# Attention and a two-layer feed-forward on one core: two score blocks side by side, one more PSUM bank for part of the first product, and loads of values begun elsewhere

## The chip, the cores and the metric

The kernel runs on one core of a Trainium2 chip. Its time is the device time of one execution in microseconds; the median of three runs is used. TensorE (PE in the profile) multiplies, VectorE (DVE) and ScalarE (ACT) work on its results, GpSimd (POOL) masks and starts loads, and SyncE (SP) starts transposing and storing transfers. All times here are microseconds unless another unit stands with them.

## The reference

Attention with 4 batches, 8 heads, 768 positions and 64 values a head. Each query sees its last 128 keys and the first 4 keys, the sinks. Its result, 3072 tokens of 512 numbers, goes through two products with a GELU of the sigmoid form between them:

```python
keep = is_sink | in_window
scores = np.where(keep, scale * np.matmul(q, k.transpose(0, 1, 3, 2)), -1e9)
a = np.exp(scores - np.max(scores, axis=-1, keepdims=True))
a = a / (np.sum(a, axis=-1, keepdims=True) + 1e-09)
x = np.matmul(a, v)          # heads are put side by side: (3072, 512)
h = x @ w_in                 # (3072, 2048)
out = (h * (1 / (1 + np.exp(-1.702 * h)))) @ w_out
```

## The kernel before

**Tiles.** A group is 256 tokens of one batch: three groups a batch, 12 in all, g = 0 to 11. Within a group, the heads go in four pairs (hp = 0 to 3) and the queries in two blocks of 128 (i). The position of the group within its batch is t = g mod 3; at t = 0 the first block has no block of keys ahead of it, so some work is smaller there.

**Steps of a group.** `load_qk` and `load_v` bring queries, keys and values as fp16 by transfers that POOL issues (L123). Queries and keys are transposed, from group 4 on by a transfer that SP issues (`transposed_qk`, L169). `sinks` computes the scores with the sink keys. `scores` computes one pair's scores into a PSUM tile `nat` of two banks: eight products that use 64 rows of the array each (L222, L224). `maxima` runs on DVE: it lays the previous block's allowed scores over the own block's (L236), takes maxima (L240) and makes the bias (L244). `weights` takes the exponentials on ACT (L255), `weights_transposed` transposes them by a transfer of SP (L275, tile `AT`), `lower` on DVE and `upper` on POOL mask them (L305, L318), `values` multiplies with the values (L332 to L344), and `normal` divides by the sums (L361, L362). `x_transposed` transposes the result by another transfer (L380). `hidden` computes one eighth of the first product (tile `hT`, eight products of 128x256) and its GELU (L397); `out_part` computes a quarter of the second product for one block of 128 tokens (four products of 128x512, L409), and `out_store` copies the result out of PSUM, on ACT for block 0 (L435) and on DVE for block 1 (L437).

**Stages.** The order is written out by hand. In stage n the attention of group n runs beside the first product of group n-1 and the second product of group n-2. `second` opens the stage: exponentials of pairs 0 and 1 on ACT, the second product of block 0, the scores of pair 2, a quarter of the second product of block 1, the scores of pair 3, and the other three quarters. Then come eight steps F2 = 0 to 7 of the first product, and between them the sinks' transpose and the scores of pairs 0 and 1 of group n+1 (F2 = 1), and the value products of the four pairs (F2 = 3, 4, 6, 7). Each engine works through its instructions in the order in which the code issues them.

**PSUM.** It has eight banks: `nat` has two buffers of two banks; the pool "mm" has two banks, for `hT` and the second product's `o`, which take turns; the pool "av" has two, for the sinks' transpose `tAs`, the sinks' scores `sk` and the value products. In stage 11, which has the first product of group 10 (NG - 2), `hidden` takes av banks for F2 = 2 and 3.

**Loads.** The queries and keys of group n+3 are issued in stage n, each load behind one of the masks of POOL. The two loads of values of group n+3 are issued in stage n too, each after a copy of one number on POOL (`paced_load`, L352) that waits for the reciprocals of pair 1 and of pair 2. The values of group 4 are loaded before stage 2.

Of the kernel before, what the change touches and what calls it, by code (L numbers as in the profile page):

```python
# [57 lines left out]
def kernel(  # L58
# [11 lines left out]
    nc = tc.nc  # L70
# [6 lines left out]
    NF = DF // P  # L77
    NT = S // TG
    NG = B * NT
# [15 lines left out]
    pace = big.tile([1, 1], FP32, name="pace")  # L95
# [13 lines left out]
    G = [dict() for _ in range(NG)]  # L109

    def load_part(g: int, part: int):


        b, t = divmod(g, NT)
        e, i = divmod(part, 2)
        rows = slice(t * TG + i * P, t * TG + (i + 1) * P)
        if part == 0:
            G[g]["qkn"] = work.tile([P, 4, DM], FP16, tag="qkn", bufs=3, name=f"qkn{g}")
        if part < 4:
            dst = G[g]["qkn"][:, part].rearrange("s (h d) -> s h d", h=H)  # L120
        else:
            dst = vn[b][t][:, i, :, 0:D]
        nc.gpsimd.dma_start(dst, (q, k, v)[e][b, :, rows].rearrange("h s d -> s h d"))  # L123
# [5 lines left out]
    def load_v(g: int):  # L129
        for part in (4, 5):  # L130
            load_part(g, part)
# [77 lines left out]
    def scores(g: int, hp: int):  # L209

        b, t = divmod(g, NT)
        qkT = G[g]["qkT"]
        nat = psp.tile([P, 2, 2, 2 * P], FP32, tag="nat", bufs=2, name=f"nat{g}_{hp}")
        for i in range(2):
            I = 2 * t + i
            prev = None if I == 0 else qkT[:, 1, 0, hp] if i else G[g - 1]["qkT"][:, 1, 1, hp]
            for part, keys in ((0, prev), (1, qkT[:, 1, i, hp])):
                for h in range(2):
                    r = bass.ts(h, D)
                    o = nat[:, h, i, bass.ts(part, P)]  # L220
                    if keys is None:
                        nc.tensor.matmul(o, masked_l[r], masked_r[r], start=True, stop=True)  # L222
                    else:
                        nc.tensor.matmul(o, qkT[r, 0, i, hp], keys[r], start=True, stop=True)  # L224
        G[g]["nat", hp] = nat

    def kinds(mask, t: int):

        m = mask.rearrange("p (i c) -> p i c", i=2)
        if t == 0:  # L230
            return m.unsqueeze(1).broadcast_to((P, 2, 2, P))
        return m[:, 1:2].unsqueeze(1).broadcast_to((P, 2, 2, P))

    def maxima(g: int, hp: int):
        nat = G[g]["nat", hp]
        nc.vector.copy_predicated(  # L236
            out=nat[:, :, :, P:], mask=kinds(take_prev, g % NT), data=nat[:, :, :, 0:P]
        )
        m1 = work.tile([P, 2, 2], FP32, tag="m1", name=f"m1{g}_{hp}")
        nc.vector.tensor_reduce(  # L240
            out=m1.rearrange("p h i -> p (h i)"), in_=nat.rearrange("p h i c -> p (h i) c")[:, :, P:],
            axis=AX.X, op=ALU.max,
        )
        nc.vector.scalar_tensor_tensor(  # L244
            out=G[g]["bias"][:, :, hp], in0=m1.rearrange("p h i -> p i h"), scalar=-scale,
            in1=G[g]["m2"][:, :, hp], op0=ALU.mult, op1=ALU.min,
        )
# [13 lines left out]
    def weights_transposed(g: int, hp: int):  # L261
        A = G[g]["A", hp]
        AT = work.tile([P, 2, 2, P], FP16, tag="AT", bufs=6, name=f"AT{g}_{hp}")
        flat = AT.rearrange("p h i s -> p (h i) s")
        if g < 3:
            bank = av_bank if g == 2 or (g, hp) == (1, 3) else mm_bank
            tp = bank(f"tA{g}_{hp}", (P, 4, P), FP16)
            for a in range(4):
                nc.tensor.transpose(tp[:, a], A[:, a], ident)
            if g == 0 or hp < (2 if g == 2 else 3):  # L270
                nc.scalar.copy(flat, tp)
            else:
                nc.vector.tensor_copy(out=flat, in_=tp)
        else:
            nc.sync.dma_start_transpose(flat, A.rearrange("p a c -> p (a c)"))  # L275
        G[g]["AT", hp] = AT
# [69 lines left out]
                )  # L346
        G[g]["av", hp] = av

    def paced_load(g: int, part: int, n: int, hp: int):

        if g < NG:
            nc.gpsimd.tensor_copy(out=pace, in_=G[n]["rcp", hp][0:1, 0, 0:1])  # L352
            load_part(g, part)

    def normal(g: int, hp: int):
        av = G[g]["av", hp]
# [27 lines left out]
    def hidden(g: int, F2: int):  # L384
        xT = G[g]["xT"]
        if F2 == 0:
            G[g]["gT"] = work.tile([P, NF, TG], FP16, tag="gT", bufs=3, name=f"gT{g}")

        bank = av_bank if g == NG - 2 and F2 in (2, 3) else mm_bank
        hT = bank(f"hT{g}_{F2}", (P, 2, 2, P))  # L390
        for f in range(2):
            F = 2 * F2 + f
            for c in range(4):
                nc.tensor.matmul(  # L394
                    hT[:, f], w_in16[:, c, bass.ts(F, P)], xT[:, :, c], start=(c == 0), stop=(c == 3)
                )
        nc.scalar.activation(  # L397
            out=G[g]["gT"][:, 2 * F2 : 2 * F2 + 2].rearrange("p f s -> p (f s)"),
            in_=hT.rearrange("p f i s -> p (f i s)"),
            func=AF.Gelu_apprx_sigmoid,  # L400
        )

    def out_part(g: int, i: int, part: int):

        if part == 0:
            G[g]["o", i] = mm_bank(f"o{g}_{i}")
        o, gT = G[g]["o", i], G[g]["gT"]
        for F in range(4 * part, 4 * part + 4):
            nc.tensor.matmul(o, gT[:, F, bass.ts(i, P)], w_out16[:, F], start=(F == 0), stop=(F == NF - 1))  # L409

    def out_last(g: int, i: int):
# [82 lines left out]
    def o(g: int, i: int, *parts):  # L494
        if 0 <= g < NG:
            for p in parts:
                out_part(g, i, p)

    def valued(g: int, hp: int):
        values(g, hp)  # L500
# [65 lines left out]


    hidden(0, 0)
    weights_transposed(1, 3)
    lower(1, 3)  # L570
# [3 lines left out]
    load_v(2)  # L574
    load_v(3)
    load_qk(4)
    load_v(4)
    hidden(0, 1)
    sink_transposed(1)
    qk_block(2, 0, by_dve)  # L580
# [49 lines left out]
    def second(n: int, g2: int, att: bool):  # L630

        if att and n + 1 < NG and (n + 1) % NT == 0:
            sink_keys((n + 1) // NT, nc.gpsimd.tensor_copy)
        if att:
            for hp in (0, 1):
                weights(n, hp)
                weights_transposed(n, hp)
        o(g2, 0, 0, 1, 2, 3)
        if att:
            scores(n, 2)  # L640
            maxima(n, 2)
        if g2 == NG - 1:
            out_store(g2, 0)
            out_last(g2, 1)
            return
        o(g2, 1, 0)
        if att:
            scores(n, 3)
            maxima(n, 3)
            sink_terms(n)  # L650
        o(g2, 1, 1, 2, 3)
        out_store(g2, 0)
        if att:
            weights(n, 2)
            weights_transposed(n, 2)
        out_store(g2, 1)
        if att:
            weights(n, 3)
            weights_transposed(n, 3)
            sink_weights(n)  # L660
            lower(n, 0)
            if n + 2 < NG:
                transposed_qk(n + 2)

    for n in range(2, NG + LAG2):
        att = n < NG
        g1, g2 = n - LAG1, n - LAG2

        if n > 2:
            second(n, g2, att)  # L670
        else:
            transposed_qk(n + 2)
        if att:
            if n > 2:
                upper(n, 0)
                upper(n, 1)
            for part in range(4):
                if n + 3 < NG:
                    load_part(n + 3, part)
                if n > 2 and part < 2:  # L680
                    upper(n, 2 + part)
        if n in (2, 3, 4):
            sink_columns(n - 1)

        for F2 in range(NF // 2):
            if 0 <= g1 < NG:
                hidden(g1, F2)
            if not att:
                continue
            if n == 2 and F2 == 0:  # L690
                weights_transposed(n, 3)
                upper(n, 3)
            if F2 == 1:
                sink_transposed(n)
                ahead(n + 1, 0)
                lower(n, 1)
                ahead(n + 1, 1)
            if F2 == 2:
                lower(n, 2)
            for hp, at in enumerate((3, 4, 6, 7) if n + 1 < NG else (4, 5, 6, 7)):  # L700
                if F2 == at:
                    values(n, hp)
                    if hp == 0:
                        lower(n, 3)
                    normal(n, hp)
                    if hp in (1, 2):
                        paced_load(n + 3, 3 + hp, n, hp)
        if att:
            x_transposed(n)
            if n + 1 < NG and (n + 1) % NT == 0:  # L710
                sink_values((n + 1) // NT)
# [34 lines left out]
```

## Time and profile before

| | |
|---|---|
| median of 3 runs | 242.43 (241.89 to 242.43) |
| the profiled execution | 242.06, of which the span is 240.3 |
| PE busy | 222.3 (93% of the span), 2220 instructions |
| ACT, DVE, POOL busy | 156.7, 147.3, 103.5 |
| hT products, L394 | 768, 95.6 busy |
| o products, L409 | 368, 85.3 busy |
| GELU, L397 | 96 of 597 ns |
| exponentials, L255 | 192 of 375 ns |
| loads of q, k and v, L123 | 72 of some 0.9 us on POOL, 5.5 to 6.2 to landing |
| DMA | 32.07 MB, 133 GB/s on average |

The busy time of PE counts each product from its start to a modelled end, and ends overlap the next starts; a product of 128x256 is shown with 275 ns though eight of them start within 0.87 us. So a share of 93% does not say that PE is near its peak, and a wait of a tenth of a microsecond is seen only in the distance between two starts. A timeline row gives the start from the beginning of the span, the duration, the engine, the line of the kernel, the operation, what it writes and reads, the shape and the number of merged instructions; brackets tell how long the engine was idle before it and what ended that.

The stages start at their first o product: stage 3 at 61.45, then 78.22, 95.85, 113.14, 129.96, 147.24, 164.92, 181.74, and stage 11 at 199.39. Each is 16.3 to 17.7 long.

### The profile page before, as it was taken

What the parts mean: (1) busy time and instruction counts of PE and PEld (TensorE: products, weight loads), DVE (VectorE), ACT (ScalarE), POOL (GpSimd) and SP (SyncE); (2) the same over time, 40 slices, a digit from 0 to 9 for tenths busy, and PEclk for the clock granted to TensorE, in tenths of its full rate; (3) what the DMA queues carried; (4) which work ended last, traced back from release to release, by engine and by line L of the source; (5) the groups of instructions that cost most, each with busy time, mean ns of one, the idle gap of its engine ahead of it and who ended that gap; (6) DMA issues with size and microseconds to landing.
All of it is one profiled execution on the core that took longest, in us unless ns stands there. A gap on an engine that the chain in (4) does not pass through costs nothing.

```text
span 240.3 us, 5810 instructions
## 1 busy us (share of the span) xinstructions
PE 222.3 (93%) x2220; PEld 155.6 (65%) x2220; DVE 147.3 (61%) x388; ACT 156.7 (65%) x356; POOL 103.5 (43%) x158
## 2 busy tenths in 40 slices
PE   1677799999999999999999999999999999999994
PEld 0454578569569469478487486585585685684863
DVE  4787947579478377477675585776692883840100
ACT  2297774884875775785776777667668658760531
POOL 8988484857237357257046057148020310310000
PEclk9999989999999999999999999999999999999999
DMA  9999999999999969989989999999982513503102
GB/s 81 148 193 193 176 207 178 154 142 148 115 154 193 137 157 172 134 158 160 151 142 153 156 165 133 172 138 125 138 196 54 148 21 65 152 5 87 46 0 87
DMA packets 130699, 32.07 MB, mean 133 GB/s; under 512 B 123120, under 2 KB 127728, under 8 KB 130672
## 3 DMA queue, kind: packets, MB, share of 16 engines
q0 software_dynamic: 79104, 13.64, 79.2%
q1 hardware_dynamic: 50992, 17.88, 41.3%
q8 instruction: 17, 0.28, 0.5%
q10 hardware_dynamic: 576, 0.20, 0.3%
q14 instruction: 10, 0.08, 0.1%
HBM read 27.50 MB, written 6.29 MB: 141 GB/s over the span
## 4 chain that ended last, share of the span: by engine, by line
PE 64%; DMA 16%; DVE 7%; ACT 5%; POOL 4%; issue 2%; SPq 1%; ACTq 0%; DVEq 0%; POOLq 0%
PE hT L394 28%; PE o L409 25%; DMA qkn<-in_k_dram 5%; DMA AT<-A 4%; DMA qkT<-qkn 4%; DMA w_in<-in_moe_w_in_dram 3%; POOL qkn L123 3%; DVE m L240 3%; DVE nat L236 3%; PE nat L224 2%; PE av L344 2%; ACT L397 2%; PE av L332 2%; PE av L340 2%; PE o L420 1%
## 5 line engine op out<-in xcount | busy, mean ns | idle before, releaser
L394 PE MATMUL hT<-xT,w_in 128*128 128x256 f16 x768 | 95.6, 275 | 1.4 <-ACT gT L397 0.9
L409 PE MATMUL o<-w_out,gT 128*128 128x512 f16 x368 | 85.3, 380 | 0.0
L397 ACT ACTIVATE gT<-hT 128x512 f16<-128x512 f32 x96 | 56.2, 597 | 41.2 <-PE hT L394 40.9
L394 PEld LDWEIGHTS <-w_in 128*128 128x128 f16 x768 | 72.8, 98 | 13.7 <-issue 1.1
L318 POOL TENSOR_SCALAR_AFFINE_SELECT up<-AT 128x512 f16<-128x512 f16 (+1 forms) x48 | 27.2, 574 | 93.6 <-DMA AT<-A 86.0
L255 ACT ACTIVATE A<-nat,bias 128x128 f16<-128x128 f32 x192 | 53.7, 375 | 18.9 <-DVE bias L244 17.3
L409 PEld LDWEIGHTS <-gT 128*128 128x128 f16 x368 | 33.6, 98 | 37.2
L236 DVE COPY_PREDICATED nat<-prev,nat 128x512 f32<-128x512 uint16 x48 | 33.3, 693 | 28.0 <-PE nat L224 17.9
L240 DVE TENSOR_REDUCE m<-nat 128x4 f32<-128x512 f32 x48 | 33.2, 691 | 1.6
L123 POOL DMA_DIRECT2D vn<-in_v_dram x24 | 21.3, 895 | 5.3 <-DMA w_out<-in_moe_w_out_dram 4.0
L123 POOL DMA_DIRECT2D qkn<-in_q_dram x24 | 21.6, 908 | 1.4 <-POOLq L727 0.8
L123 POOL DMA_DIRECT2D qkn<-in_k_dram x24 | 21.3, 893 | 2.2 <-DMA w_in<-in_moe_w_in_dram 1.7
L362 DVE TENSOR_TENSOR xn<-av,rcp 128x256 f16<-128x256 f32 x48 | 20.4, 425 | 1.7
L305 DVE TENSOR_TENSOR lo<-AT,own 128x512 f16<-128x512 f16 (+1 forms) x48 | 18.7, 412 | 2.3 <-DMA AT<-A 2.3
L340 PE MATMUL av<-vn,up 128*128 128x65 f16 x160 | 18.3, 195 | 0.0
L344 PE MATMUL av<-vn,lo 128*128 128x65 f16 x160 | 18.3, 196 | 0.0
L361 DVE RECIPROCAL rcp<-av 128x4 f32<-128x4 f32 x48 | 8.6, 179 | 14.6 <-PE av L344 14.5
L332 PE MATMUL av<-vs,AsT 128*128 128x130 f16 x80 | 16.5, 224 | 0.5 <-DVE qkT L153 0.3
L224 PEld LDWEIGHTS <-qkT 64*128 64x128 f16 x352 | 11.7, 100 | 7.4 <-issue 6.6
L224 PE MATMUL nat<-qkT 64*128 64x128 f16 x288 | 16.5, 232 | 0.0
L340 PEld LDWEIGHTS <-up 128*128 128x128 f16 x160 | 14.8, 100 | 1.2 <-issue 0.4
L397 ACT ACT_TABLE_LOAD x11 | 14.1, 1283 | 0.2
(58 smaller groups left out, 179.3 us busy)
## 6 DMA issues: line engine op xcount, KB each, us to landing
out_dram<-osb SPq DMA_DIRECT2D x23, 256.0 KB
qkn<-in_q_dram POOLq DMA_DIRECT2D x24, 128.0 KB, 5.6
qkn<-in_k_dram POOLq DMA_DIRECT2D x24, 128.0 KB, 5.5
vn<-in_v_dram POOLq DMA_DIRECT2D x24, 128.0 KB, 6.2
w_in<-in_moe_w_in_dram POOLq DMA_DIRECT2D x4, 512.0 KB, 9.9
w_out<-in_moe_w_out_dram POOLq DMA_DIRECT2D x4, 512.0 KB, 12.4
AT<-A SPq DMA_TRANSPOSE x36
xT<-xn SPq DMA_TRANSPOSE x10
```

The costliest lines, as they stand in the source:

```text
L123: nc.gpsimd.dma_start(dst, (q, k, v)[e][b, :, rows].rearrange("h s d -> s h d"))
L224: nc.tensor.matmul(o, qkT[r, 0, i, hp], keys[r], start=True, stop=True)
L236: nc.vector.copy_predicated(out=nat[:, :, :, P:], mask=kinds(take_prev, g % NT), data=nat[:, :, :, 0:P])
L240: nc.vector.tensor_reduce(out=m1.rearrange("p h i -> p (h i)"), in_=nat.rearrange("p h i c -> p (h i) c")[:, :, P:], axis=AX.X, op=ALU.max,)
L255: nc.scalar.activation(out=A[:, 2 * h + i], in_=nat[:, h, i, P:], func=AF.Exp, bias=bias[:, i, hp, h : h + 1], scale=scale,)
L318: nc.gpsimd.affine_select(out=out, in_=in_, pattern=[[0, rows], [-1, P]], compare_op=ALU.is_gt, fill=zero_reg, base=0, channel_multiplier=1,)
L332: nc.tensor.matmul(av[:, i].rearrange("p h d -> p (h d)"), AsT, vs[b][:, c : c + 2].rearrange("p h d -> p (h d)"), start=True, stop=False,)
L340: nc.tensor.matmul(av[:, i, h], up[:, h, i], vn[b][J // 2][:, J % 2, head], start=False, stop=False)
L344: nc.tensor.matmul(av[:, i, h], own_w[:, h, i], vn[b][t][:, i, head], start=(I == 0), stop=(I == 0 or h == 1))
L394: nc.tensor.matmul(hT[:, f], w_in16[:, c, bass.ts(F, P)], xT[:, :, c], start=(c == 0), stop=(c == 3))
L397: nc.scalar.activation(out=G[g]["gT"][:, 2 * F2 : 2 * F2 + 2].rearrange("p f s -> p (f s)"), in_=hT.rearrange("p f i s -> p (f i s)"), fun ...
L409: nc.tensor.matmul(o, gT[:, F, bass.ts(i, P)], w_out16[:, F], start=(F == 0), stop=(F == NF - 1))
```

## The change

Three edits. In `second`, the scores of pair 2 and pair 3 are issued one right behind the other, after two products of block 1 instead of before its first quarter and after it; the maxima of both follow. In `hidden`, the step F2 = 2 takes its bank from "av" instead of "mm" for groups 2 to 9 (group 10 keeps F2 = 2 and 3). And the values of group n+2 (instead of n+3) are loaded in `second` of stage n, behind one copy on POOL that waits for the last exponential of pair 1; the values of group 4 are loaded in stage 2, behind its loads of queries and keys. `out_part` takes a range of products instead of the number of a quarter.

```diff
-    def paced_load(g: int, part: int, n: int, hp: int):
+    def paced_values(g: int, n: int):
         if g < NG:
-            nc.gpsimd.tensor_copy(out=pace, in_=G[n]["rcp", hp][0:1, 0, 0:1])
-            load_part(g, part)
+            nc.gpsimd.tensor_copy(out=pace, in_=G[n]["A", 1][0:1, 3, 0:1])
+            load_v(g)
...
-        bank = av_bank if g == NG - 2 and F2 in (2, 3) else mm_bank
+        more = (2,) if 2 <= g < NG - 2 else (2, 3) if g == NG - 2 else ()
+        bank = av_bank if F2 in more else mm_bank
...
     load_qk(4)
-    load_v(4)
     hidden(0, 1)
...
             for hp in (0, 1):
                 weights(n, hp)
                 weights_transposed(n, hp)
+            paced_values(n + 2, n)
         o(g2, 0, 0, 1, 2, 3)
-        if att:
-            scores(n, 2)
-            maxima(n, 2)
...
-        o(g2, 1, 0)
+        out_part(g2, 1, 0, 2)
         if att:
+            scores(n, 2)
             scores(n, 3)
+            maxima(n, 2)
             maxima(n, 3)
             sink_terms(n)
-        o(g2, 1, 1, 2, 3)
+        out_part(g2, 1, 2, NF)
...
+        if n == 2:
+            load_v(4)
...
-                    if hp in (1, 2):
-                        paced_load(n + 3, 3 + hp, n, hp)
```

More of the change, by code (lines that the diff above doesn't have):

```diff
@@ L401, in hidden, with out_part @@
         )
-    def out_part(g: int, i: int, part: int):
-        if part == 0:
+    def out_part(g: int, i: int, F0: int, F1: int):
+        if F0 == 0:
             G[g]["o", i] = mm_bank(f"o{g}_{i}")
         o, gT = G[g]["o", i], G[g]["gT"]
-        for F in range(4 * part, 4 * part + 4):
+        for F in range(F0, F1):
             nc.tensor.matmul(o, gT[:, F, bass.ts(i, P)], w_out16[:, F], start=(F == 0), stop=(F == NF - 1))
@@ L496, in o @@
             for p in parts:
-                out_part(g, i, p)
+                out_part(g, i, 4 * p, 4 * p + 4)
     def valued(g: int, hp: int):
```

## The prediction

> **What bounds the kernel now.** I read the page first, then the PE timeline of one stage, then DVE, ACT and POOL in the same stretch.
>
> ```profile
> PE 222.3 (93%) x2220; PEld 155.6 (65%) x2220; DVE 147.3 (61%) x388; ACT 156.7 (65%) x356; POOL 103.5 (43%) x158
> ...
> PE 64%; DMA 16%; DVE 7%; ACT 5%; POOL 4%; issue 2%; SPq 1%; ACTq 0%; DVEq 0%; POOLq 0%
> ```
>
> TensorE carries 64% of the chain that ended last, and no other engine comes near. Its ends are modelled, so a short stall does not show as idle; it shows between starts. Stage n=6 (113.14 to 129.96), PE alone:
>
> ```profile
> 113.14 3.62 PE L409 MATMUL o<-w_out,gT 128*128 128x512 f16 x16
> 116.69 0.23 PE L222 MATMUL nat<-maskedr,maskedl 64*128 64x128 f16 x2
> 116.76 0.33 PE L224 MATMUL nat<-qkT 64*128 64x128 f16 x6
> 117.02 1.04 PE L409 MATMUL o<-w_out,gT 128*128 128x512 f16 x4
> 117.99 0.23 PE L222 MATMUL nat<-maskedr,maskedl 64*128 64x128 f16 x2
> 118.06 0.33 PE L224 MATMUL nat<-qkT 64*128 64x128 f16 x6
> 118.32 2.76 PE L409 MATMUL o<-w_out,gT 128*128 128x512 f16 x12
> 120.92 1.98 PE L394 MATMUL hT<-xT,w_in 128*128 128x256 f16 x16
> ...
> 123.07 0.23 PE L224 MATMUL nat<-qkT,qkT 64*128 64x128 f16 x2
> ...
> 123.30 0.22 PE L224 MATMUL nat<-qkT,qkT 64*128 64x128 f16 x2
> 123.36 0.33 PE L224 MATMUL nat<-qkT 64*128 64x128 f16 x6
> 123.76 1.91 PE L394 MATMUL hT<-xT,w_in 128*128 128x256 f16 x16
> ```
>
> The reader is to see three things. (1) Twelve o products that no scores follow take 118.32 to 120.92, 0.2165 each; the four ahead of scores take 117.02 to 117.99, 0.97 instead of 0.866: 0.10 is lost going into the scores. (2) From the last row of scores to the next product is 0.26 (116.76 to 117.02) when nothing is awaited, but 0.40 (123.36 to 123.76) ahead of the third hT: 0.14 is a wait. (3) The two hT blocks from 120.92 end where the next work starts, at 122.73 (1.81); 16 products at 0.109 (the blocks of eight without a wait take 0.87, 108.58 to 109.45) make 1.74, so 0.07 is a wait of the second block. The rows that end these waits:
>
> ```profile
> 118.73 0.69 DVE L236 COPY_PREDICATED nat<-prev,nat 128x512 f32<-128x512 uint16 x1
> 119.46 0.69 DVE L240 TENSOR_REDUCE m<-nat 128x4 f32<-128x512 f32 x1
> 120.19 0.16 DVE L244 SCALAR_TENSOR_TENSOR bias<-m,m 128x4 f32<-128x4 f32 x1
> 120.38 0.23 DVE L281 TENSOR_TENSOR ts<-bias,sn 128x64 f32<-128x64 f32 x1
> 121.12 0.69 DVE L437 COPY osb<-o 128x512 f32<-128x512 f32 x1 [0.51 <-PE o L409]
> ```
>
> ```profile
> 123.12 1.08 ACT L397 ACTIVATE gT<-hT 128x512 f16<-128x512 f32 x2
> ```
>
> The first GELU ends at 123.12 + 0.60 = 123.72, and the third hT starts at 123.76: it wants that mm bank. The second hT wants the bank that the osb copy (121.12 to 121.81) empties. The GELU itself hangs on scores, maxima, exponentials and a table load, all behind the scores of pair 3.
>
> **The change, part by part** (times in stage 6; the others alike, where I say nothing).
>
> *Adjacent scores.* One trip into and out of the scores goes. A single block with its trip costs 0.97 - 0.866 + 0.33 = 0.435; a second block right behind another costs 0.23 (the step 123.07 to 123.30 between the two blocks further on). Saved: 0.20 a stage, in the nine stages n=3 to 11. But pair 2 now starts two products later, 0.43, and the maxima run on DVE back to back: 118.73 becomes 119.16, the last bias 120.62, ts 120.81, and DVE is free for the osb copy at about 121.0. That copy could start at 120.92 (its product is done 0.20 earlier), so it starts near 121.0, 0.12 earlier than 121.12. The second hT, which waits for it, gains **0.12**, not 0.20; the rest becomes a longer wait there. Pair 3 is asked for sooner, at 117.35; its nat buffer is free when the eight exponentials end at 117.06 (114.89 + 2.17), 0.29 ahead, and in stages 4, 7 and 10, where ACT is 0.11 later, 0.17 ahead. I cost that wait at nothing; if that cover goes, each 0.1 counts in full.
>
> *Third bank.* The third hT takes the av bank that the sinks' transpose used; it waits for the copy AsT, which ended at 123.22, instead of the GELU. Its wait goes: 0.14 in stages 5 to 9, by the same reading 0.09 in stage 3, 0.50 in stage 4 and 0.51 in stage 10, where one delay of 0.36 on DVE had pushed the GELU back. Stage 11 had the bank already. Late next is the fourth hT, which wants the first GELU: that now ends 0.43 later, 124.15, and the fourth hT starts at 123.76 - 0.26 + 0.87 = 124.37. No new wait, 0.2 to spare. The second value product (126.62) now waits for the third GELU, over by 125.4.
>
> *Loads of values.* The same loads, 0.89 of POOL each, leave the end of the stage before (128.61 and 129.88 in stage 6, for group 9) and go behind the eighth exponential, about 117.2 to 119.1, for group n+2; the pace copies fall from 14 to 7 (0.23 each). Behind them on POOL stand up of pairs 0 and 1, the q loads, up of 2 and 3, and the k loads. Up 0 ran at 118.89 here, later in stages 7 to 9, so it moves little, and its value products come at 125.5. No load is near its use (two stages). In stage 2, two loads of 0.89 come ahead of up 3 (57.35 to 59.1, done 59.8); its products start at 61.09: 1.3 to spare. What the move changes is traffic: the value loads no longer share the engines with xT and the first A transposes, but may with the third and fourth. One stage pays for a late fourth one now:
>
> ```profile
> 162.31 0.43 DVE L305 TENSOR_TENSOR lo<-AT,own 128x512 f16<-128x512 f16 x1 [0.82 <-DMA AT<-A]
> ...
> 163.34 0.22 PE L332 MATMUL av<-vs,AsT 128*128 128x130 f16 x1 [0.24 <-DVE xn L362]
> ```
>
> In stage 8 the transpose landed 15.05 after the stage's start and PE lost 0.40. Where the first q load was issued early (7.6 into the stage, n=3 and 5) it landed at 12.7 to 12.8; where late (9.1), at 13.0 to 15.1. The move lets up 1, and so the q load, go early again. I count the 0.40 as saved.
>
> *Sum:* 5 x 0.26 + 0.21 + 0.62 + 0.63 + 0.12 + 0.40 = 3.3.
>
> *What takes from it.* DVE no longer has 0.5 to spare ahead of the osb copy, and POOL disturbs it. Stage 10:
>
> ```profile
> 188.79 0.53 DVE L244 SCALAR_TENSOR_TENSOR bias<-m,m 128x4 f32<-128x4 f32 x1
> ```
>
> ```profile
> 188.67 0.63 POOL L318 TENSOR_SCALAR_AFFINE_SELECT up<-AT 128x512 f16<-128x512 f16 x1 [0.67 <-DMA AT<-A]
> ```
>
> A bias that takes 0.16 took 0.53 under an up. Today only stage 10's costs PE anything (the others fall into the 0.5); after the change every one delays the osb copy, and so PE. In the stage's own time the biases move to 5.94 and 7.47 and ts to 7.66; up 0 can start when the value loads are issued, about 6.0, and up 1 when its transpose lands, 6.8 to 7.3. In stages 10 and 11, which load no values, up 0 runs from 5.6 to 6.2, over the first bias. A stage can lose nothing or all of an up (0.63; 0.40 in n=3, 6, 9). I take 0.14, a quarter: the starts are spread and mostly miss. Nine stages: 1.3. **Gain 2.0.**
>
> The Trainium skill (SBUF — State Buffer, Who interferes with whom) speaks against the change here: a VectorE instruction with two SBUF inputs and a GpSimd one that reads SBUF exclude each other, whoever starts first holding the port for its whole length. The rows above agree (0.53 for 0.16). By it a start of up just ahead of the bias would cost its full length, and the sum would be that of rival 1.
>
> The profiled execution took 242.06 for a span of 240.3; it lies between the shown runs (241.89 to 242.43, median 242.43). 242.06 - 2.0 = **240.1**.
>
> **Rivals.**
> 1. *DVE held in most stages.* For: up follows its transpose, and its new slot is set by the loads, right at the bias. Against: stages 3, 6 and 9 have the short form, and a bias that starts first is not hurt (stage 11: 0.16, with up 0.04 behind). At 0.33 a stage, 3.3 - 3.0 = 0.3: 241.8.
> 2. *The value loads stand ahead of the fourth A transpose* (slower). For: in stage 9 the first transpose landed at 9.41, right behind a value load at 9.26, after 6.46 instead of the 2.41 it takes in stage 10. Against: issued at 4.2 and 5.1, the loads should be down by 8 to 10, and the transpose is issued at 9.05. It decides from a landing of 14.4 into the stage (stage 8's 15.05 - 0.40 - 0.26). If one load's 0.95 (spacing of landings in the backlog around 45) is added to today's 13.0 to 15.1, the mean is 15.0 and the stall 0.6, in seven stages 4.2: 242.06 - 3.3 + 4.2 = 243.0.
> 3. *The third bank is none*: the third hT waits for AsT as long as it did for GELU, since AsT stands behind the product lo on DVE, which waits for a transpose. Against: even stage 9's late one let AsT start at 9.85, on time. Only the osb gain, 9 x 0.12, would be left: 241.0.
>
> **How the numbers follow.** A measurement of this kernel can tell about 0.3%, 0.73, from no change, so faster means below 241.7. Forecast 0.67; rival 1 0.15; rival 2 0.10; rival 3 0.08. Faster: forecast and rival 3, less the forecast's slow edge, 0.74; same, rival 1 and that edge, 0.15; slower 0.11. The range runs from no collision at all (238.8, and 0.2 for the scatter) to rival 1 with 0.35 a stage (242.0); only rival 2 and the tails lie outside.
>
> **What would show it.** In a stage: the scores of pairs 2 and 3 are 0.23 apart; the step from the last scores to the third hT is 0.26; the osb copy starts at about 7.85 into the stage; the second hT waits some 0.2; the fourth hT does not wait; stages 3 to 10 are 16.5 to 17.2 long. Wrong if pair 3 waits for ACT, if bias or ts take 0.4 or more in most stages, or if PE waits at a value product for lo or xn.

## The result, and the profile after

| | before | changed |
|---|---|---|
| median of 21 runs | 242.43 (241.44 to 243.74) | 241.56 (240.42 to 242.89) |
| profiled execution, its span | 242.06, 240.3 | 240.97, 239.2 |
| ratio | | 0.9964, 95% interval 0.9949 to 0.998 |

The change gains 0.87, or 0.36%; 2.0 from the profiled execution, 2.3 from the median, had been forecast. The page's line on the chain of work that ended last, which the prediction shows of the kernel before:

```profile
PE 71%; DVE 13%; DMA 7%; ACT 3%; issue 2%; POOL 1%; SPq 0%; DVEq 0%; POOLq 0%
```

PE's share of the chain rose from 64 to 71% and DVE's from 7 to 13%. The chain names what was followed last, not what was lost; that is read stage by stage. Length of each stage, from its first o product to the next stage's:

| stage | 3 | 4 | 5 | 6 | 7 | 8 | 9 | 10 | 11 | sum |
|---|---|---|---|---|---|---|---|---|---|---|
| before | 16.76 | 17.64 | 17.29 | 16.82 | 17.28 | 17.68 | 16.82 | 17.65 | 16.31 | 154.25 |
| changed | 16.67 | 16.98 | 18.62 | 16.53 | 17.16 | 18.13 | 16.52 | 17.23 | 16.21 | 154.05 |

Seven stages are shorter, stages 5 and 8 longer, and the sum moves by 0.20. Of the 1.09 between the two profiled executions, 0.89 lies ahead of stage 3: the changed kernel's began it at 60.56, the one before at 61.45, and the twelve experiments at 60.9 to 61.5. One profile is one execution, so the medians decide whether a kernel is faster, and the profiles say where the time went.

A stage that went as intended, stage 6 on PE:

```profile
112.83 4.05 PE L411 MATMUL o<-w_out,gT 128*128 128x512 f16 x18
116.81 0.23 PE L222 MATMUL nat<-maskedr,maskedl 64*128 64x128 f16 x2
...
117.04 0.22 PE L222 MATMUL nat<-maskedr,maskedl 64*128 64x128 f16 x2
...
122.88 0.33 PE L224 MATMUL nat<-qkT 64*128 64x128 f16 x6
123.14 1.92 PE L396 MATMUL hT<-xT,w_in 128*128 128x256 f16 x16
```

The two score blocks stand 0.23 apart, and from the last scores to the third hT it is 0.26 (123.14 - 122.88) where it was 0.40. The stage became 0.29 shorter.

Stage 5 is where it went wrong. SP, POOL, DVE and PE in turn:

```profile
103.14 0.53 SPq L441 DMA_DIRECT2D out_dram<-osb  x1
103.77 1.22 SPq L275 DMA_TRANSPOSE AT<-A  x1
```

```profile
103.00 0.89 POOL L123 DMA_DIRECT2D qkn<-in_q_dram  x1
```

```profile
110.22 0.43 DVE L305 TENSOR_TENSOR lo<-AT,own 128x512 f16<-128x512 f16 x1 [1.82 <-DMA AT<-A]
```

```profile
111.25 0.22 PE L332 MATMUL av<-vs,AsT 128*128 128x130 f16 x1 [1.37 <-DVE xn L362]
```

The stage starts at 94.21. The fourth transpose of the exponentials is issued on SP behind a store, 9.56 into the stage (9.13 before), and the first load of queries (the q load from here on) had been issued 0.77 ahead of it. The two land together, the load 15.87 and the transpose 15.98 into the stage. DVE waits 1.82 for the transpose with its product lo, the normalising behind it comes late, and the third value product, which needs the av bank that this empties, starts 1.54 after its usual distance from the hT block ahead of it (the 1.37 of the view leaves out PE's modelled end). The same costs 0.60 in stage 8 and 0.15 in stage 3: **2.29** in all, where the kernel before lost 0.40.

The second loss, 0.06 to 0.55 a stage, is at the second hT. Stage 8, DVE and POOL:

```profile
152.46 0.72 DVE L244 SCALAR_TENSOR_TENSOR bias<-m,m 128x4 f32<-128x4 f32 x1
```

```profile
152.50 0.66 POOL L318 TENSOR_SCALAR_AFFINE_SELECT up<-AT 128x512 f16<-128x512 f16 x1
```

A bias that takes 0.16 alone takes 0.72 beside a mask; the next maxima, ts and the osb copy come 0.55 late, and the second hT with them. Against the wait of 0.12 that stages 3, 4, 6 and 9 have there, stages 5, 7, 8, 10 and 11 lose 0.10, 0.18, 0.55, 0.25 and 0.06: **1.14**.

So the 0.20 is what is left of 3.6 gained (0.20 + 1.14 + 2.29) when the losses of 1.1 and 2.3 are taken off.

### The profile page after: what moved, and what is told of

It reads as the page before. It is cut to its first block, busy times and chain, and to the rows that moved or that the text cites. A ratio compares the mean times of both kernels' runs of the same rounds, so it can differ in the third digit from the quotient of the medians.

```text
span 239.2 us, 5783 instructions
## 1 busy us (share of the span) xinstructions
PE 220.3 (92%) x2220; PEld 155.4 (65%) x2220; DVE 145.3 (61%) x388; ACT 155.7 (65%) x356; POOL 103.3 (43%) x151
## 4 chain that ended last, share of the span: by engine, by line
PE 71%; DVE 13%; DMA 7%; ACT 3%; issue 2%; POOL 1%; SPq 0%; DVEq 0%; POOLq 0%
PE hT L396 29%; PE o L411 27%; DMA AT<-A 5%; PE nat L224 4%; DVE m L240 4%; DVE nat L236 4%; PE av L344 2%; ACT A L255 2%; PE av L332 2%; DMA qkn<-in_k_dram 2%; PE av L340 2%; PE o L422 1%; DVE xn L362 1%; PE tA L269 1%; DVE osb L439 1%
## 5 line engine op out<-in xcount | busy, mean ns | idle before, releaser
L411 PE MATMUL o<-w_out,gT 128*128 128x512 f16 x368 | 83.8, 379 | 0.0
L399 ACT ACTIVATE gT<-hT 128x512 f16<-128x512 f32 x96 | 55.1, 597 | 37.4 <-PE hT L396 37.2
L411 PEld LDWEIGHTS <-gT 128*128 128x128 f16 x368 | 34.3, 98 | 38.4
L318 POOL TENSOR_SCALAR_AFFINE_SELECT up<-AT 128x512 f16<-128x512 f16 (+1 forms) x48 | 28.3, 593 | 66.5 <-DMA AT<-A 59.4
L305 DVE TENSOR_TENSOR lo<-AT,own 128x512 f16<-128x512 f16 (+1 forms) x48 | 17.8, 387 | 4.7 <-DMA AT<-A 4.7
L361 DVE RECIPROCAL rcp<-av 128x4 f32<-128x4 f32 x48 | 8.6, 179 | 11.4 <-PE av L344 11.2
L224 PE MATMUL nat<-qkT 64*128 64x128 f16 x288 | 15.1, 228 | 0.0
```

Of the source, the lines that this page charges most:

```text
L318: nc.gpsimd.affine_select(out=out, in_=in_, pattern=[[0, rows], [-1, P]], compare_op=ALU.is_gt, fill=zero_reg, base=0, channel_multiplier=1,)
L399: nc.scalar.activation(out=G[g]["gT"][:, 2 * F2 : 2 * F2 + 2].rearrange("p f s -> p (f s)"), in_=hT.rearrange("p f i s -> p (f i s)"), fun ...
```

## The experiments

Theory A: the moved loads of values make the fourth transpose late. B: the adjacent scores do, by issuing it 0.43 later. C: what is missing went to masks that hold DVE. D, formed after the first four runs: the moved loads and the later issue make it late only together. All ratios are to the kernel before, run on the same chip; the figures in brackets are 95% intervals.

### The parts alone

**e1.** Adjacent scores alone, against the kernel before (`out_part` takes its bounds as in the change):

```diff
-        if att:
-            scores(n, 2)
-            maxima(n, 2)
...
-        o(g2, 1, 0)
+        out_part(g2, 1, 0, 2)
         if att:
+            scores(n, 2)
             scores(n, 3)
+            maxima(n, 2)
             maxima(n, 3)
             sink_terms(n)
-        o(g2, 1, 1, 2, 3)
+        out_part(g2, 1, 2, NF)
```

> The adjacent scores alone; third hT in its old mm bank, loads as before. Theory A and B alike: the scores of pair 2 start 0.43 later, so the first GELU ends 0.42 later (10.99 into the stage for 10.57), and the third hT, which wants that bank, starts with it: six stages lose 0.42 to 0.47, stages 4 and 10 about 0.05, stage 11 gains 0.1: slower by about 2.5, ratio 1.010 (1.007 to 1.014). Rival (each edit gives its own share): 9 x 0.12 faster, ratio 0.9955.

Measured: 245.52, ratio 1.0112 (1.0083 to 1.014). Stage 5, PE:

```profile
107.89 1.91 PE L394 MATMUL hT<-xT,w_in 128*128 128x256 f16 x16 [0.68 <-ACT gT L397]
```

The third hT waits for the first GELU, now openly. Alone, the edit that saves PE two switches a stage costs 1.1%.

**e2.** The bank alone, against the kernel before:

```diff
-        bank = av_bank if g == NG - 2 and F2 in (2, 3) else mm_bank
+        more = (2,) if 2 <= g < NG - 2 else (2, 3) if g == NG - 2 else ()
+        bank = av_bank if F2 in more else mm_bank
```

> The third bank alone. The third hT's waits of the trace before go: 5 x 0.14 + 0.09 + 0.50 + 0.51 = 1.8 faster, ratio 0.9925 (0.990 to 0.995). Rival (the av bank is no freer than the mm bank, or the DMA paces the stages): no change, 0.999 to 1.001.

Measured: 241.11, 0.9945 (0.9916 to 0.9974). Its profile has stages 6, 9, 4 and 10 shorter by 0.13, 0.13, 0.49 and 0.50 as expected, and 0.98 lost at a value product of stage 8: the fourth transpose landed 15.49 into it, behind a q load issued 0.51 ahead, with neither the moved loads nor a later issue (9.13).

**e3.** The loads alone, against the kernel before (`load_v(4)` moves as in the change):

```diff
                 weights_transposed(n, hp)
+            paced_values(n + 2, n)
...
-                    if hp in (1, 2):
-                        paced_load(n + 3, 3 + hp, n, hp)
```

> The moved loads of values alone. Theory A (the loads, issued some 4.2 to 6 into the stage, stand ahead of the third and fourth transposes of the exponentials and make PE wait at a value product): slower by 0.5 to 2, ratio 1.002 to 1.008, with waits in stages 5 and 8. Theory B (the fourth transpose is late because adjacent scores issue it 0.43 later): the loads alone cost nothing, or gain stage 8's 0.4: ratio 0.998 to 1.000.

Measured: 241.71, 0.9962 (0.9942 to 0.9981): neither theory's answer, a gain. Value products did wait, 0.25, 0.31 and 0.51 in stages 3, 5 and 8, so the traffic is there. In its profile a gain stands against that: the third hT of stages 4 and 10 waits 0.36 less, since a delay on DVE in these stages is gone. The two nearly cancel (a stage sum of 154.22), and the gain of the median is not seen in this one execution.

**e4.** Scores and bank, loads as before: the two diffs of the scores and the bank together, or, against the changed kernel:

```diff
-            paced_values(n + 2, n)
...
+                    if hp in (1, 2):
+                        paced_load(n + 3, 3 + hp, n, hp)
```

> Adjacent scores and third bank, loads as before. Theory A: without the moved loads the gain is that of the sum, about 2.2, ratio 0.991 (0.989 to 0.993). Theory B: the fourth transpose is issued at 9.5 instead of 9.1 all the same, PE waits at value products in stages 7 and 8, and the gain is no larger than that of the whole change: 0.995 to 0.998. Theory C (POOL's masks hold DVE): 0.993 to 0.996 with bias or ts of 0.4 and more in most stages.

Measured: 240.64, 0.9921 (0.9891 to 0.9951). Theory B falls: the later issue alone leaves a gain of 1.8 in place (242.48 for the kernel before beside it), with one wait of 0.33 at a value product. The second hT loses 1.50 here, 0.36 of it in stage 4 to a delay on DVE beside which no mask ran, so the loss at the second hT comes with the adjacent scores and not with the moved loads. So 0.9962 for the loads and 0.9921 for the rest make 0.9964 together, where the product would be 0.988: the parts work against each other. That is theory D, though e2 and e3 show that a single edit can make this transpose late in some stages too.

### The two losses, cured one at a time

**e5.** The second store put behind the fourth transpose, the rest as changed (this diff and those that follow are against the changed kernel):

```diff
-        out_store(g2, 1)
         if att:
             weights(n, 3)
             weights_transposed(n, 3)
             sink_weights(n)
+        out_store(g2, 1)
+        if att:
             lower(n, 0)
```

> The changed kernel, with the fourth transpose of the exponentials issued on SP ahead of the store of block 1 instead of behind it. Theory D (adjacent scores issue that transpose 0.43 later, at 9.5 to 10 into the stage, and moved loads put the first q load just ahead of it; together it comes too late in stages 5 and 8, where PE waited 1.54 and 0.60 at a value product): it is issued at about 9.1, lands 0.4 to 0.9 earlier, and 0.5 to 1.2 come back: ratio to before 0.992 to 0.9945 (the change: 0.9964). Theory C (what is missing was lost to POOL's masks holding DVE): no change, 0.996 to 0.997.

Measured: 240.09, 0.9916 (0.989 to 0.9942). Stage 5 (start 94.83), SP and then DVE:

```profile
102.45 2.66 SPq L275 DMA_TRANSPOSE AT<-A  x2
105.20 0.53 SPq L441 DMA_DIRECT2D out_dram<-osb  x1
```

```profile
108.79 0.74 DVE L305 TENSOR_TENSOR lo<-AT,own 128x512 f16<-128x512 f16 x2
```

The transposes of pairs 3 and 4 go out in one run, the last at 9.08 into the stage, and it lands at 13.25 instead of 15.98; both products lo run without a wait. In the view of waits, what DVE waited for that transpose (in total, times, longest), in the changed kernel and in this one:

```profile
DVE lo L305 <- DMA AT<-A: 4.7, 5, 1.8
```

```profile
DVE lo L305 <- DMA AT<-A: 0.7, 1, 0.7
```

An order of two issues on SP gives back about 1.2 (by the ratios) to 1.5 (by the medians); 0.9916 lies clear of the changed kernel's interval. The q load was still issued 0.17 ahead of the transpose and landed sooner too, at 12.80 instead of 15.87, so which of the transfers held up which is not shown.

**e12.** Whether the order as such is worth something, late transpose or not, is asked of the kernel before with the same edit:

```diff
-        out_store(g2, 1)
         if att:
             weights(n, 3)
...
             sink_weights(n)
+        out_store(g2, 1)
```

> The kernel before with nothing but the fourth transpose ahead of the store. Its lateness cost it stage 8's 0.4 at most: ratio 0.998 to 1.000. If the order on SP is worth 0.4% or more here too, then its gain in the changed kernel says nothing of the change.

Measured: 242.44, 0.9993 (0.9969 to 1.0018). No gain like that of e5. The 0.40 at the value product of stage 8 did go, but in this profile stage 7 lost as much to a bias and ts beside masks; a gain of 0.40, 0.17%, could not be told from none in the median.

**e6.** No loads of values, values of batch 0 for all:

```diff
-    load_v(3)
...
-            paced_values(n + 2, n)
...
-                        av[:, i, h], up[:, h, i], vn[b][J // 2][:, J % 2, head], start=False, stop=False
+                        av[:, i, h], up[:, h, i], vn[0][J // 2][:, J % 2, head], start=False, stop=False
```

> The changed kernel without the loads of values of groups 3 to 11 and their pace copies: every batch is multiplied with the values of batch 0, so the output is not the reference's. Theory A or D (the traffic of loads makes the fourth transpose late): no wait at a value product, ratio 0.988 to 0.991. If the first q load alone does it, whatever the values do: waits in stages 5 and 8 stay, 0.994 to 0.996. Theory C: the first mask starts earlier, over the first bias as in stage 10 (0.25 a stage), 0.995 to 0.997.

Measured: 240.11, 0.9915 (0.9886 to 0.9943). The time is nearly that of the first answer, but the waits at value products did not go: 0.45 in stage 5, 0.45 in stage 6, 0.08 in stage 8. Here the q load went out early (7.6 into stage 5) and met the third transpose, which took 4.2 to land, and the fourth behind it landed at 14.86. So the value loads are not the only ones: a q load issued close to these transposes goes with a late landing without them too. Theory A in its narrow form falls as well.

**e7.** All loads of queries and keys behind the fourth mask:

```diff
-                upper(n, 0)
-                upper(n, 1)
+                for hp in range(4):
+                    upper(n, hp)
             for part in range(4):
                 if n + 3 < NG:
                     load_part(n + 3, part)
-                if n > 2 and part < 2:
-                    upper(n, 2 + part)
```

> The changed kernel, with all four loads of queries and keys issued behind the fourth mask instead of between the masks. Theory D: the fourth transpose no longer meets a q load, lands by 12.5, and no value product waits for it: ratio 0.991 to 0.994. Rival (the late loads make xT and the first transposes of the next stage late instead, which then hold the first product): 0.996 or above, with waits ahead of the first hT. Theory C: as the change, 0.996 to 0.997.

Measured: 239.84, 0.9908 (0.9886 to 0.9931). No value product waits more than 0.06 in its profile, and the first hT does not wait either: the same loss cured from the other side, by taking the q load out of the transpose's way. The second hT still loses 1.12, as in the changed kernel, so this run parts the two losses.

**e8.** The first mask behind ts:

```diff
             if n > 2:
+                nc.gpsimd.tensor_copy(out=pace, in_=G[n]["ts"][0:1, 0, 0:1])
                 upper(n, 0)
```

> The changed kernel, with one copy on POOL ahead of the first mask that waits for ts, so that no mask runs over the biases and ts. Theory C: the 1.1 that the second hT lost in stages 5, 7, 8, 10 and 11 (0.10, 0.18, 0.55, 0.25, 0.06) comes back: ratio 0.991 to 0.993. Theory D: that 1.1 comes back at the second hT, but the q loads go out later, nearer to the fourth transpose, and the waits at value products grow: 0.994 to 0.998.

Measured: 239.85, 0.990 (0.9877 to 0.9923). A little faster than either answer, as e5 and e7 were. The second hT's wait is 0.18 to 0.19 in stages 5 to 10, and 0.55 in stage 11, where the osb copy starts 0.4 late for a reason that is not shown. The biases are back at 0.16. Against 0.12 that is still 0.86 lost, for 1.14 in the changed kernel. But the q load moved too (9.59 into stage 5, behind the transpose's issue at 9.47), and the waits at value products shrank to 0.27 in stage 4 and 0.21 in stage 5 with it. So most of what this run gains in its profile comes from the transposes (2.29 down to 0.48), and 0.28 from the masks.

### Both cures

**e9.** The transpose first, and the first mask behind ts:

```diff
-        out_store(g2, 1)
         if att:
             weights(n, 3)
...
             sink_weights(n)
+        out_store(g2, 1)
...
+                nc.gpsimd.tensor_copy(out=pace, in_=G[n]["ts"][0:1, 0, 0:1])
                 upper(n, 0)
```

> The changed kernel with two of the earlier edits: fourth transpose ahead of the store, and first mask behind ts. If the two losses (late fourth transpose, masks over the biases) are separate, both come back: stages 3 to 11 sum to 151 to 151.5, ratio to before 0.985 to 0.988. If both edits only cure the same loss: as each alone, 0.990 to 0.992.

Measured: 239.31, 0.987 (0.9841 to 0.99). With the transpose first alone it was 240.09, 0.9916 (0.989 to 0.9942). The intervals overlap a little, so a further gain of the second edit is likely, not shown. The profiles do not show it: the nine stages take 151.62 here and 151.48 in e5, whose profiled execution was among the fastest of its twelve (239.07 of 239.04 to 242.42).

**e10.** With the loads of queries and keys behind the masks in addition:

```diff
+                nc.gpsimd.tensor_copy(out=pace, in_=G[n]["ts"][0:1, 0, 0:1])
-                upper(n, 0)
-                upper(n, 1)
+                for hp in range(4):
+                    upper(n, hp)
...
-                if n > 2 and part < 2:
-                    upper(n, 2 + part)
```

> The edits of the run before, and all loads of queries and keys behind the fourth mask. Nothing late is left: 0.985 to 0.987. If the loads there make xT or the next first transposes late: 0.988 or above, with waits ahead of the first hT.

Measured: 239.24, 0.9859 (0.9828 to 0.9889): the fastest median of all (238.56 to 239.61 in six runs), though its interval overlaps that of the run ahead of it. Stage 5, POOL and DVE:

```profile
102.81 0.17 POOL L677 COPY pace<-ts 1x1 f32<-1x1 f32 x1 [1.82 <-DVE ts L281]
102.94 1.40 POOL L318 TENSOR_SCALAR_AFFINE_SELECT up<-AT 128x512 f16<-128x512 f16 x2
```

```profile
102.18 0.16 DVE L244 SCALAR_TENSOR_TENSOR bias<-m,m 128x4 f32<-128x4 f32 x1
102.45 0.23 DVE L281 TENSOR_TENSOR ts<-bias,sn 128x64 f32<-128x64 f32 x1
```

The masks start when the second bias and ts are done. The nine stages take 151.51, 2.7 less than before.

### What the moved loads are worth

**e11.** Scores, bank and the transpose first, loads as before:

```diff
-            paced_values(n + 2, n)
...
-        out_store(g2, 1)
         if att:
             weights(n, 3)
...
             sink_weights(n)
+        out_store(g2, 1)
...
+                    if hp in (1, 2):
+                        paced_load(n + 3, 3 + hp, n, hp)
```

> Adjacent scores, third bank and the fourth transpose ahead of the store; loads as before. If the moved loads are worth something once their harm is cured, this stands behind the changed kernel with the same cure (0.9916): 0.992 to 0.994. If they are worth nothing: 0.990 to 0.992, since the two alone gave 0.9921 with one value product's wait of 0.3.

Measured: 241.70, 0.9954 (0.9924 to 0.9984), slower than either answer, against 0.9916 with the loads moved, on different chips. In its profile the value loads in their old place are issued 0.22 ahead of stage 7 and 0.78 into it, just ahead of xT. PE and SP:

```profile
138.56 1.16 PE L396 MATMUL hT<-xT,w_in 128*128 128x256 f16 x9 [1.90 <-DMA xT<-xn]
```

```profile
129.80 1.23 SPq L380 DMA_TRANSPOSE xT<-xn  x1
```

xT took 8.7 to land, and the first hT was 2.07 late; in the changed kernel xT lands by 5.8 into every stage. So the move relieves the transposes at a stage's start and burdens those in its middle. What it is worth stays open: the intervals with and without it overlap (0.9924 to 0.9942), and e4, which keeps the loads in their old place without the other order on SP, reached 0.9921, no worse than 0.9916.

## Why the prediction was wrong

**Right: the mechanism on PE.** The score blocks of pairs 2 and 3 stand 0.23 apart, the osb copy starts at 7.82 into an undisturbed stage (7.85 forecast), the step to the third hT is 0.26, the fourth hT never waits, and the undisturbed stages 6 and 9 became 0.29 and 0.30 shorter (0.26 forecast). Pair 3 never waited for ACT. Gross gain: 3.6, against 3.3. What a later GELU does without the bank, 1.1%, came as worked out (e1).

**Right in size: masks over the biases.** 1.3 was taken, 1.14 read from the trace, though in five stages and once at 0.55, so that the size was in part luck. That a bias which starts first is not hurt, by stage 11 of before, did not hold: stage 8's was shown 0.04 ahead of the mask, as stage 11's had been, and took 0.72. By the Trainium skill (SBUF — State Buffer, Who interferes with whom) whichever of the two issues first holds the shared port for its whole length. The trace agrees in the length, since bias and mask end 0.02 apart (153.18 and 153.16), but a distance of 0.04 between starts did not tell which one would wait.

**Wrong by 2.3: the step on traffic**, "The move lets up 1, and so the q load, go early again. I count the 0.40 as saved." Three things in it failed. The second transpose was to land at 6.8 to 7.3 and let up 1 go; beside the value loads, issued at the same time, it landed at 8.0 to 11.4. So the q load went out at 8.8 to 12.1, not at 7.6, and in stages 3, 5, 7 and 8 just ahead of the fourth transpose. And that transpose was held to be "issued at 9.05", though it was issued at 9.13 to 9.33 before and in the working its exponentials had moved by 0.43; behind them and the store, which takes SP 0.53, it went out at 9.44 to 9.97. Its landing at up to 15.98 cost 2.29 of waits in place of 0.40 saved. The step promised nothing left, so it is off by 2.29. The stages of the profiles miss 1.8 of the forecast (0.2 for 2.0); this step takes 2.3, and the other two terms, the gain on PE (0.3 better than forecast) and the masks (0.2 better), give 0.5 back.

**The rivals.** Rival 2 named the mechanism and the point of decision, about 14.4 into the stage: landings of 14.40, 15.98 and 15.50 cost 0.15, 1.54 and 0.60; the others, at 14.17 and less, nothing. It had seven stages stall by 0.6 each and a chance of 0.10; three did, by 0.8 on average, which ends at a small gain and not at a loss. Rival 1 happened with rival 2, at some 0.4 of its size (1.14 of 3.0). They were set against the forecast one at a time; at the sizes measured they took 3.4 together, and the stages came out at almost no change. Rival 3 is refuted by e2. In the chances, rival 1 with the forecast's edge of 0.01 makes 0.16, not 0.15.

**How the runs carry it.** The waits of PE in every profile with adjacent scores and the third bank, read as distances between starts (second hT: what goes beyond 0.12):

| | at value products | at the second hT | at the first hT | stages 3 to 11 | ratio of medians |
|---|---|---|---|---|---|
| changed | 2.29 | 1.14 | 0 | 154.05 | 0.9964 |
| e4, loads as before | 0.33 | 1.50 | 0.36 | 152.82 | 0.9921 |
| e5, transpose first | 0.34 | 0.51 | 0 | 151.48 | 0.9916 |
| e6, no values | 0.98 | 0.98 | 0 | 152.59 | 0.9915 |
| e7, loads behind masks | 0.11 | 1.12 | 0 | 151.88 | 0.9908 |
| e8, masks behind ts | 0.48 | 0.86 | 0 | 151.95 | 0.990 |
| e9, e5 and e8 | 0.16 | 0.84 | 0 | 151.62 | 0.987 |
| e10, e9 and e7 | 0.03 | 0.86 | 0 | 151.51 | 0.9859 |
| e11, e4 and transpose first | 0.42 | 1.42 | 2.06 | 154.54 | 0.9954 |

In all nine the stages take 150.63 and these waits, to within 0.02, so nothing else was lost in them. e5 and e7 remove the late transpose in two ways and reach 0.9916 and 0.9908, clear of the changed kernel's interval; e7 does so with the loss at the second hT left as it was. e12 shows no such gain where the transpose was late in one stage only. That the late fourth transpose took most of what is missing is shown by this; why it and the q load beside it land so late in some stages is not. What the masks cost the median is not shown: e8 to e10 take only 0.3 of the second hT's 1.14 away, and lose 0.07 in each of stages 5 to 10 and 0.42 to 0.44 in stage 11 instead. The forecast of 240.1 is near what e5 measures (240.09), a kernel with this one loss cured.

## What to carry to other kernels

An edit that starts one thing later moves everything behind it on every queue, the issue of a transfer on SP too: follow the moved work until its last transfer has landed, and only then count what it hid. A load put into a quiet stretch takes that quiet from the transfer that used it. So list what is in flight beside each transfer that a later step waits for, and try issuing that one ahead of stores, as in e5. And two edits that each gain alone have still to be run together.

## What was not expected of the hardware

A transpose of exponentials lands 2.4 to 2.6 after its issue in stages 10 and 11 of the changed kernel, which have no loads (one of the eight took 3.45), and up to 7.05 beside loads (the second of stage 4). In the four stages in which the q load was issued just ahead of the fourth transpose, the two landed within 0.4 of each other (14.38 and 14.40, 15.87 and 15.98, 13.78 and 14.17, 15.11 and 15.50).

The first q load takes longer in stages 5 and 8: 7.1 and 6.1 to landing in the changed kernel, 4.2 to 5.1 in 3, 6 and 7 (6.4 in stage 4, where it was issued last, at 12.12); 6.4 and 6.3 with the loads alone (e3). Stages 5 and 8 load the third group of a batch. Why it takes longer there was not tried.

In stage 4 the second COPY_PREDICATED started 0.36 late in all six kernels with the loads of values in their old place (at 5.95 where the scores of pair 2 come first, at 6.38 with adjacent scores) and in none of the eight without (5.59 and 6.02). No mask ran then. What held DVE is open.
